# Moving the layer-norm gradient behind the state sums in a fused S4 and feed-forward gradient kernel

## The chip, the cores and the metric

One Trainium2 chip, and one of its cores. The metric is the device time of one execution of the kernel in microseconds. In what follows PE is the matrix engine, DVE the vector engine, ACT the scalar engine, POOL the GpSimd engine and SP the sync engine, which here issues most of the DMAs. Each engine runs its instructions in the order of its own queue.

## The reference

The kernel computes a block and all its gradients: a layer norm, whose result goes through a long convolution with an S4 state-space kernel and, beside it, through a feed-forward layer that gates it. The input has 2048 rows of 512, the feed-forward layer has 1792 units, and the state has 128 entries per channel.

```python
xn = _layernorm(x)                     # x = A_u, 2048 x 512
K  = einsum("dn,dnl,dn->dl", Cc, exp(logdA[:, :, None] * l), dB).real
s  = causal convolution of xn with K, by FFT  + xn * Dskip
g  = silu(silu(xn @ w1) @ w2)          # 512 -> 1792 -> 512
out = x + s * g
# returned: out, and the gradients of A_u, A_re, A_im, B_re, B_im, C_re, C_im, log_dt, Dskip, w1, w2
```

The change touches three parts of the gradient. The *state sums* turn the gradient of `K` into those of A, B, C and `log_dt`. The *weight gradients* are those of `w2` and `w1`, two products over all 2048 rows. The *norm gradient* adds up the two gradients that reach `xn` (from the convolution and from the feed-forward layer), takes them through the layer norm, and adds the gradient that came in: with y the summed gradient of a row, its result is `rstd * (y - mean(y) - xn * mean(y * xn)) + grad_out`.

## The kernel before, in words

The kernel is written as Python generators. Each `yield` ends a *step*, and helpers mix the steps of several generators: `interleave` gives each generator a number of steps per round, `paced(gen, other, rate)` runs `rate` steps of `other` for each step of `gen`, and `chained` runs generators one after another. What comes out is an order of priority. The framework that builds the program then puts the instructions of each engine in order by this priority and by when it reckons that each is ready, so that the queues keep the order of the steps only roughly. It also adds the waits on semaphores. Tiles with a tag rotate through `bufs` buffers, and a new use of a buffer waits for the last reader of the old one. A pool that is opened in memory of a closed pool waits in the same manner, tile by tile.

The forward part, the gradient of the convolution and the gradient through the feed-forward layer (`gen_ffn_da`) come first and are not changed. The state sums start beside `gen_ffn_da`. In the profiled execution the last call of the kernel function, line 1147, takes over at about 545 us. It mixes three things:

- `gen_ssm_bwd` (L825), the state sums, 16 groups in all, of which about ten are still to come. For each group, `ssm_turned` (L722) loads `YT` with two DMA transposes on SP; `ssm_v` (L729) makes 16 matmuls, which ACT evicts to `Vb` in four pieces; `ssm_products` (L742) forms `Tp` by four multiplications on DVE; and `ssm_sums` (L752) adds up `Tp` by 43 matmuls with an identity, evicted by ACT to `Sa`. A group's matmuls are placed one step, its products one group, and its sums two groups after it has begun. For every second group `ssm_half` (L711) makes `Gb` on DVE and loads `Eb`; for every fourth, `ssm_fold` (L682) loads `GE` and makes `Gf`. After every fourth group `gen_ssm_grads` (L766) turns `Sa` into the gradients of A, B, C and `log_dt`: some 45 small DVE instructions, six PE transposes (`pt_g`, L813), a matmul for `log_dt` (`pd`, L818), one more DVE instruction (`ddt`, L820), and stores on POOL.
- `gen_dw2` (L911) and then `gen_dw1` (L943), the weight gradients. Each of 14 steps of `gen_dw2` loads an `h_in` (512 KB, SP), transposes one in 16 PE instructions (`pt_t`, L118), applies SiLU on ACT to make `a_tok` (two instructions), multiplies in 16 matmuls of 512 columns (L936), evicts on ACT to `o11`, and stores on POOL. `gen_dw1` loads, for each of 7 blocks, a `dh_tok` by two DMA transposes on SP (L949; two buffers), and makes four steps of 16 matmuls of 256 columns each (L954), evicts each on ACT, and stores the block on POOL. All these evictions are line 44 in the profile, and these products share three PSUM buffers. The profile calls both output tiles `o`, as it does the `o1` below.
- `gen_ln_bwd` (L961), the norm gradient, in 8 chunks of 256 rows. `load` fetches `du` (gradient from the convolution), `pd_l` (from the feed-forward layer) and `Gt` (the incoming gradient), 256 KB each, on SP. `sums` forms the sum and the two means on DVE (L983, L984, each twice, and a short L985) and scales the sum on ACT (L988, twice). `rows` puts the result together on DVE (L994 twice, L995) and stores it on POOL (L996). `rows` of a chunk follows `sums` of the next.

```python
    interleave([ssm, chained([gen_dw2(k, fw), gen_dw1(k, fw)]), after(8, gen_ln_bwd(k, fw))], [2, 1, 2])
```

The round is two steps of the state sums, one of the weight gradients and two of the norm gradient, which is held back for eight steps. The norm gradient therefore runs out after 13 rounds, in the middle of the state sums; the state sums end while `gen_dw1` is at its first block; and the other 27 steps of `gen_dw1`'s 28 run with nothing beside them. All tiles of the norm gradient lie in the pool `fw`, beside those of the weight gradients. The tiles of the state sums lie in `sb`, on the other side of the memory, which stays open until the kernel ends.

Of the kernel before, what the change touches and what calls it, by code (L numbers as in the profile page):

```python
# [13 lines left out]
BF16 = mybir.dt.bfloat16  # L14
# [3 lines left out]
P = 128  # L18
# [29 lines left out]
def interleave(gens, weights=None):  # L48
    gens = list(gens)
    weights = list(weights or [1] * len(gens))  # L50
    alive = [True] * len(gens)
    while any(alive):
        for i, g in enumerate(gens):
            if not alive[i]:
                continue
            for _ in range(weights[i]):
                try:
                    next(g)
                except StopIteration:
                    alive[i] = False  # L60
                    break
# [16 lines left out]
def chained(gens):  # L78
    for g in gens:
        yield from g  # L80


def after(n, g):
    for _ in range(n):
        yield
    yield from g
# [9 lines left out]
def paced(gen, other, rate):  # L96

    n = 0.0
    for _ in gen:
        n += rate  # L100
        while n >= 1:
            next(other, None)
            n -= 1
# [9 lines left out]
def turned(k, src, n, out, ev):  # L113

    for i in range(0, n, 8):
        pt = k.pf.tile([P, 8, P], BF16, name="pt_t", tag="pf")
        for j in range(8):
            k.nc.tensor.transpose(out=pt[:, j], in_=src(i + j), identity=k.ident[:])  # L118
        ev(out[:, i:i + 8], pt[:])
# [705 lines left out]
def gen_ssm_bwd(k, sb):  # L825


    par = load_params(k, sb, 0, k.D)
    par["dt"] = k.dt[:]
    groups = [(b, h, q0) for b in range(4) for h in range(2) for q0 in (0, 8)]  # L830
    gf, half, yt, vb, tp, S, tail = {}, {}, {}, {}, {}, {}, []
    gf[0] = ssm_fold(k, 0, sb)
    yt[0] = ssm_turned(k, *groups[0], sb)
    yield
    n = len(groups)
    for i in range(n + 2):
        if i < n:
            b, h, q0 = groups[i]
            if q0 == 0:
                half[i // 2] = ssm_half(k, b, h, gf[b], sb)  # L840
            if i + 1 < n:
                yt[i + 1] = ssm_turned(k, *groups[i + 1], sb)
            vb[i] = ssm_v(k, q0, half[i // 2][0], yt.pop(i), sb)
            if (i % 4) == 2 and b < 3:
                gf[b + 1] = ssm_fold(k, b + 1, sb)
            yield
        if i >= 2:
            j = i - 2
            b, h, q0 = groups[j]
            if (j % 4) == 0:  # L850
                S[b] = sb.tile([P, 3, 32, 2, 4], F32, name="Sa", tag="Sa", bufs=2)
            ssm_sums(k, tp.pop(j), S[b][:, :, 16 * h + q0:16 * h + q0 + 8])
            yield
            if (j % 4) == 3:
                tail.append(gen_ssm_grads(k, b, S.pop(b), par, sb))
        if 1 <= i <= n:
            tp[i - 1] = ssm_products(k, groups[i - 1][2], vb.pop(i - 1), half[(i - 1) // 2][1], sb)
            yield
        if tail:
            if next(tail[0], "end") == "end":  # L860
                tail.pop(0)
    for t in tail:
        yield from t
# [47 lines left out]
def gen_dw2(k, fw):  # L911
    nc = k.nc

    def load(ft):
        h = fw.tile([P, k.T, P], BF16, name="h_in", tag="h_in", bufs=2)
        nc.sync.dma_start(h[:].rearrange("p t n -> p (t n)"), k.Hd[ft])
        return h

    def turn(h):
        a = fw.tile([P, k.T, P], BF16, name="a_tok", tag="a_tok", bufs=2)  # L920
        turned(k, lambda t: h[:, t], k.T, a, lambda out, in_: nc.scalar.activation(out=out, in_=in_, func=ACT.Silu))
        return a
    h = load(0)
    yield
    a = turn(h)
    h = load(1)
    yield
    for ft in range(k.FT):
        at = a
        if ft + 1 < k.FT:  # L930
            a = turn(h)
            if ft + 2 < k.FT:
                h = load(ft + 2)
        ps = k.pf.tile([P, k.D], F32, name="ps_w2", tag="pf")
        for t in range(k.T):
            nc.tensor.matmul(out=ps[:], lhsT=at[:, t, :], rhs=k.do[:, t, :], start=(t == 0), stop=(t == k.T - 1))  # L936
        ob = fw.tile([P, k.D], BF16, name="o11", tag="o11", bufs=2)
        k.evb(ob[:], ps[:])
        k.st(k.outs[11][ft * P:ft * P + P, :], ob[:])  # L939
        yield  # L940


def gen_dw1(k, fw):  # L943
    nc = k.nc
    o10 = k.outs[10].rearrange("(k p) f -> p k f", p=P)
    for f in range(k.FT // 2):
        dh = fw.tile([P, k.T, 2, P], BF16, name="dh_tok", tag="dh_tok", bufs=2)
        for j in range(2):
            nc.sync.dma_start_transpose(dh[:, :, j, :], k.DHd[2 * f + j])  # L949
        ob = fw.tile([P, k.DK, 256], BF16, name="o10", tag="o10", bufs=2)  # L950
        for dk in range(k.DK):
            ps = k.pf.tile([P, 256], F32, name="ps_w1", tag="pf")
            for t in range(k.T):
                nc.tensor.matmul(out=ps[:], lhsT=k.xn[:, t, dk * P:dk * P + P], rhs=dh[:, t].rearrange("p j n -> p (j n)"),  # L954
                                 start=(t == 0), stop=(t == k.T - 1))
            k.evb(ob[:, dk], ps[:])
            yield
        k.st(o10[:, :, 256 * f:256 * f + 256], ob[:])  # L958


def gen_ln_bwd(k, lw):  # L961
    nc = k.nc
    TT, STT = nc.vector.tensor_tensor, nc.vector.scalar_tensor_tensor
    D = k.D
    n = k.T // 2
    cols = lambda ap: ap.rearrange("p (b d) -> p b d", b=4)

    def load(c):
        du = lw.tile([P, 4, 2, P], BF16, name="du", tag="du", bufs=3)
        nc.sync.dma_start(du[:].rearrange("p b t d -> p b (t d)"), k.dUd[:, :, 256 * c:256 * c + 256].rearrange("b p n -> p b n"))  # L970
        pd = lw.tile([P, 2, D], BF16, name="pd_l", tag="pd_l", bufs=3)
        nc.sync.dma_start(pd[:], k.Pd[:, 2 * c:2 * c + 2, :])
        Gt = lw.tile([P, 2, D], BF16, name="Gt", tag="Gt", bufs=2)
        nc.sync.dma_start(Gt[:], k.g_v[:, 2 * c:2 * c + 2, :])
        return du, pd, Gt

    def sums(c, du, pd, Gt):

        m = lw.tile([P, 2, 4], F32, name="m", tag="m", bufs=2)
        for i in range(2):  # L980
            t = 2 * c + i
            jk = lw.tile([P, D], BF16, name="jk", tag="jk", bufs=1)
            STT(out=cols(pd[:, i]), in0=cols(pd[:, i]), scalar=1.0, in1=du[:, :, i, :], op0=ALU.mult, op1=ALU.add, accum_out=m[:, i, 0:1])  # L983
            STT(out=jk[:], in0=pd[:, i], scalar=1.0, in1=k.xn[:, t, :], op0=ALU.mult, op1=ALU.mult, accum_out=m[:, i, 1:2])  # L984
        STT(out=m[:, :, 2:4], in0=m[:, :, 0:2], scalar=-1.0 / D,  # L985
            in1=k.rstd[:, 2 * c:2 * c + 2].unsqueeze(2).to_broadcast([P, 2, 2]), op0=ALU.mult, op1=ALU.mult)
        for i in range(2):
            nc.scalar.activation(out=pd[:, i], in_=pd[:, i], func=ACT.Identity, scale=k.rstd[:, 2 * c + i:2 * c + i + 1], bias=m[:, i, 2:3])  # L988
        return pd, Gt, m

    def rows(c, pd, Gt, m):
        o1 = lw.tile([P, 2, D], BF16, name="o1", tag="o1", bufs=2)
        for i in range(2):
            STT(out=o1[:, i], in0=k.xn[:, 2 * c + i, :], scalar=m[:, i, 3:4], in1=Gt[:, i], op0=ALU.mult, op1=ALU.add)  # L994
        TT(out=o1[:], in0=o1[:], in1=pd[:], op=ALU.add)  # L995
        k.st(k.o1_v[:, 2 * c:2 * c + 2, :], o1[:])  # L996
    q, pend = [load(0)], None
    for c in range(n + 1):
        if c + 1 < n:
            q.append(load(c + 1))  # L1000
        yield
        cur = sums(c, *q.pop(0)) if c < n else None
        yield
        if pend:
            rows(c - 1, *pend)
        pend = cur


@with_exitstack
def kernel(ctx, tc, A_u, A_A_re, A_A_im, A_B_re, A_B_im, A_C_re, A_C_im, A_log_dt, A_Dskip, B_x, B_w1, B_w2, grad_out,  # L1010
           out_0, out_1, out_2, out_3, out_4, out_5, out_6, out_7, out_8, out_9, out_10, out_11):
    nc = tc.nc
    k = KCtx()
    k.nc, k.tc = nc, tc
    k.outs = [out_0, out_1, out_2, out_3, out_4, out_5, out_6, out_7, out_8, out_9, out_10, out_11]
    L, D, F = A_u.shape[1], A_u.shape[2], B_w1.shape[1]
# [7 lines left out]
    def pool(name, side=None, es=ctx, **kw):  # L1024
        kw.setdefault("bufs", 1)
        return es.enter_context(tc.tile_pool(name=name, side=side, reuse_waits="tile", **kw))
# [111 lines left out]
    ffb = gen_ffn_da(k, da)  # L1138
    paced(bwd, woven([ffb, out], [2, 1]), BR)
    es_x.close()  # L1140
    sb = pool("sb", side="right")
    ssm = gen_ssm_bwd(k, sb)
    paced(ffb, ssm, SR)
    run(out)
    es_d.close()
    fw = pool("fw")
    interleave([ssm, chained([gen_dw2(k, fw), gen_dw1(k, fw)]), after(8, gen_ln_bwd(k, fw))], [2, 1, 2])
# [1 line left out]
_INS = ['A_u', 'A_A_re', 'A_A_im', 'A_B_re', 'A_B_im', 'A_C_re', 'A_C_im', 'A_log_dt', 'A_Dskip', 'B_x', 'B_w1', 'B_w2', 'grad_out']  # L1149
_OUTS = [((1, 2048, 512), 'bfloat16'), ((1, 2048, 512), 'bfloat16'), ((512, 128), 'bfloat16'), ((512, 128), 'bfloat16'), ((512, 128), 'bfloat16'), ((512, 128), 'bfloat16'), ((512, 128), 'bfloat16'), ((512, 128), 'bfloat16'), ((512,), 'bfloat16'), ((512,), 'bfloat16'), ((512, 1792), 'bfloat16'), ((1792, 512), 'bfloat16')]  # L1150
# [25 lines left out]
```

## Time and profile before

| what | value |
|---|---|
| median of 6 runs | 732.91 us (730.46 to 741.04) |
| profiled execution | 734.1 us, of which the profile's span is 732.4 |
| PE busy | 601.7 us (82% of the span), 5500 matmuls |
| DVE busy | 553.3 us (76%) |
| ACT busy | 496.8 us (68%) |
| POOL busy | 100.3 us (14%) |
| mean granted TensorE clock | 0.936 |
| DMA | 159.26 MB, mean 217 GB/s |
| last matmul of `gen_dw1` begins its group of 128 | 710.14 us, for 14.13 us |

All times in the profile count from the start of the span. Matmuls are pipelined: a busy PE need not be at its peak, and a matmul's own duration is longer than the distance from one to the next. For the rate, the length of a whole group is used. Where a line shows an idle time in square brackets, it is the time that the engine stood still ahead of the instruction, with the instruction or DMA that ended it. Such a wait costs the kernel time only if the engine decides when the kernel ends, or if one that does is waiting for it.

### The profile page before, as it was taken

The page shows a single profiled execution, that of the slowest core. Times are in us where ns is not written, and L with a number is a line of the kernel's source. Part 1 is how long each engine was busy: PE and PEld are TensorE (multiplying, and loading weights), DVE is VectorE, ACT ScalarE, POOL GpSimd, SP SyncE. Part 2 cuts the span into 40 slices and gives each one's busy share as a digit, 9 for nine tenths or more (in the row PEclk, how much of TensorE's full clock was granted, in tenths as well). Part 3 has the DMA queues.
Part 4 walks back from the last instruction along what each step waited for, and adds up shares of the span by engine and source line. Part 5 has one row for each costly group of instructions (what it writes and reads, how often), then busy time and mean ns, then how long its engine had stood idle before and what let it go on. Part 6 is the DMA issues. An engine that isn't in the chain of part 4 may idle for free.

```text
span 732.4 us, 13942 instructions
## 1 busy us (share of the span) xinstructions
PE 601.7 (82%) x5500; PEld 433.5 (59%) x5500; DVE 553.3 (76%) x1070; ACT 496.8 (68%) x671; POOL 100.3 (14%) x180
## 2 busy tenths in 40 slices
PE   0667968969999875669798999989897978999895
PEld 0435646555665653445575676758676656666784
DVE  6969996869988749976896999746897897794100
ACT  7768759679889866858788787636746866661211
POOL 2172100000010026200000000000002103102300
PEclk9978989999999995879999999999999989999998
DMA  9877847769679976569988865599979999930872
GB/s 286 316 168 193 271 170 206 271 179 299 251 194 254 351 256 165 193 149 256 322 217 262 239 208 197 151 219 219 213 159 281 258 281 274 228 117 28 160 183 57
DMA packets 207042, 159.26 MB, mean 217 GB/s; under 512 B 129024, under 2 KB 185344, under 8 KB 203392
## 3 DMA queue, kind: packets, MB, share of 16 engines
q1 hardware_dynamic: 193856, 135.29, 70.1%
q0 software_dynamic: 6224, 18.10, 6.9%
q10 hardware_dynamic: 6896, 4.98, 2.2%
q8 instruction: 43, 0.70, 0.4%
q14 instruction: 23, 0.19, 0.1%
HBM read 65.14 MB, written 62.26 MB: 174 GB/s over the span
## 4 chain that ended last, share of the span: by engine, by line
issue 52%; DVE 5%; POOL 4%; DMA 3%; PE 0%; ACT 0%; POOLq 0%; ACTq 0%; SPq 0%; DVEq 0%
DMA out_dram<-o 2%; POOL out_dram L939 1%; DMA Kd<-KE 1%; DVE YD L599 1%; POOL out_dram L816 1%; DMA Gr<-in_grad_out_dram 1%; DVE sp_in L332 1%; DVE ds L595 1%; POOL out_dram L631 1%; POOL out_dram L958 1%; POOL out_dram L996 1%; DVE sp_in L337 0%; POOL g L598 0%; DVE YD L603 0%; DVE YD L601 0%
## 5 line engine op out<-in xcount | busy, mean ns | idle before, releaser
L44 ACT CAST dA<-ps_s 128x1024 bf16<-128x1024 f32 x96 | 94.6, 1040 | 16.3 <-PE ps_s L298 8.7
L310 PE MATMUL ps_i<-I,sp_in 128*128 128x256 bf16 x384 | 55.2, 291 | 17.5 <-ACT dK L44 7.7
L893 PE MATMUL ps_da<-doT,W 128*128 128x256 bf16 x448 | 60.7, 280 | 4.8 <-ACT doT L44 2.9
L541 PE MATMUL ps_h<-XT,W 128*128 128x256 bf16 x448 | 62.4, 290 | 1.5 <-ACT hT L44 0.9
L558 PE MATMUL ps_o<-W,aT 128*128 128x512 bf16 x224 | 57.9, 398 | 3.1 <-ACT aT L549 2.9
L310 PEld LDWEIGHTS <-sp_in 128*128 128x128 bf16 x384 | 38.0, 103 | 33.5 <-DVE sp_in L333 16.7
L44 ACT CAST o<-ps_w 128x256 bf16<-128x256 f32 (+1 forms) x42 | 18.6, 443 | 57.8 <-PE ps_w L954 42.4
L44 ACT CAST dB<-ps_i 128x1024 bf16<-128x1024 f32 x48 | 47.2, 1025 | 15.7 <-PE ps_i L310 13.3
L746 DVE TENSOR_TENSOR Tp<-Vb,Eb 128x1344 bf16<-128x1344 bf16 x64 | 52.4, 852 | 3.9 <-PE psS L762 3.4
L904 PE MATMUL ps_dx<-W,dhT 128*128 128x512 bf16 x224 | 53.8, 379 | 0.0
L893 PEld LDWEIGHTS <-W 128*128 128x128 bf16 x448 | 44.5, 101 | 14.5 <-issue 5.8
L541 PEld LDWEIGHTS <-W 128*128 128x128 bf16 x448 | 45.7, 104 | 12.4 <-issue 2.3
L936 PE MATMUL ps_w<-YD,a_tok 128*128 128x512 bf16 x224 | 52.3, 386 | 0.7 <-ACT o L44 0.7
L954 PE MATMUL ps_w<-dh_tok,xn 128*128 128x256 bf16 x448 | 50.4, 273 | 2.6 <-DMA dh_tok<-DHd 2.2
L895 DVE SCALAR_TENSOR_TENSOR dhT<-dhT,ps_da 128x512 bf16<-128x512 bf16 x56 | 37.6, 682 | 16.3 <-PE ps_da L893 16.0
L44 ACT CAST Vb<-ps_v 128x672 bf16<-128x672 f32 x64 | 42.8, 724 | 9.4 <-PE ps_v L736 9.3
L954 PEld LDWEIGHTS <-xn 128*128 128x128 bf16 x448 | 43.3, 98 | 8.4 <-issue 3.6
L297 PE MATMUL ps_s<-dB,F 128*128 128x512 bf16 x96 | 37.6, 398 | 7.0 <-DMA dB<-dA 4.3
L286 PEld LDWEIGHTS <-TF 128*128 128x128 bf16 x384 | 27.2, 105 | 26.2 <-issue 14.6
L419 ACT ACTIVATE sn<-V 128x1024 bf16<-128x1024 int32 (+3 forms) x40 | 35.1, 898 | 7.1 <-DVE V L417 6.9
L298 PE MATMUL ps_s<-dB,F 128*128 128x512 bf16 x96 | 36.8, 389 | 1.7 <-DMA dB<-dA 1.7
L447 PEld LDWEIGHTS <-YD 128*128 128x128 bf16 x512 | 24.5, 102 | 22.8 <-DVE YD L434 11.8
(220 smaller groups left out, 1371.4 us busy)
## 6 DMA issues: line engine op xcount, KB each, us to landing
Yd<-YD SPq DMA_DIRECT2D x8, 1024.0 KB, 5.8
sp_in<-Ud SPq DMA_DIRECT2D x8, 1024.0 KB, 7.1
h_in<-Hd SPq DMA_DIRECT2D x14, 512.0 KB, 5.0
Ed<-E SPq DMA_DIRECT2D x8, 672.0 KB, 5.1
Eb<-Ed SPq DMA_DIRECT2D x8, 672.0 KB, 5.8
Hd<-hT POOLq DMA_DIRECT2D x8, 512.0 KB, 7.1
Ud<-dA SPq DMA_DIRECT2D x4, 1024.0 KB, 9.4
KXd<-dA SPq DMA_DIRECT2D x4, 1024.0 KB, 6.1
```

The lines of the kernel that those rows point to most:

```text
L44: return self.nc.scalar.copy(out=out, in_=in_)
L297: nc.tensor.matmul(out=ps[:, 4 * u:4 * u + 4], lhsT=F2[:, m0], rhs=B[:, 0, g0:g0 + 4, :], start=True, stop=False)
L298: nc.tensor.matmul(out=ps[:, 4 * u:4 * u + 4], lhsT=F2[:, m1], rhs=B[:, 1, g0:g0 + 4, :], start=False, stop=True)
L310: nc.tensor.matmul(out=ps[:, g], lhsT=Y[:, c, g0 + g, :], rhs=k.I2[:, c].rearrange("p c m -> p (c m)"), start=(c == 0), stop=(c == 1))
L541: nc.tensor.matmul(out=ps[:, j], lhsT=k.W1[:, dk, ft * P:ft * P + P], rhs=XTv[:, :, dk, :], start=(dk == 0), stop=(dk == DK - 1))
L558: nc.tensor.matmul(out=ps[:], lhsT=aT[:, ft, t * P:t * P + P], rhs=k.W2[:, ft, :], start=(ft == 0), stop=(ft == FT - 1))
L746: k.nc.vector.tensor_tensor(out=Tp[:, c, :, r ^ c].rearrange("p e (q w) a -> p q w e a", w=2), in0=Vb[:, :, c].rearrange("p q w (e a) -> p ...
L893: nc.tensor.matmul(out=ps[:, j], lhsT=k.W2[:, ft, dk * P:dk * P + P], rhs=dTv[:, :, dk, :], start=(dk == 0), stop=(dk == DK - 1))
L895: nc.vector.scalar_tensor_tensor(out=dh[:, i0:i0 + 2, :], in0=dh[:, i0:i0 + 2, :], scalar=1.0, in1=ps[:], op0=ALU.add, op1=ALU.mult)
L904: nc.tensor.matmul(out=ps[:], lhsT=dhs[ft // 8][:, ft % 8, t * P:t * P + P], rhs=k.W1[:, :, ft * P:ft * P + P], start=(ft == 0), stop=(ft ...
L936: nc.tensor.matmul(out=ps[:], lhsT=at[:, t, :], rhs=k.do[:, t, :], start=(t == 0), stop=(t == k.T - 1))
L954: nc.tensor.matmul(out=ps[:], lhsT=k.xn[:, t, dk * P:dk * P + P], rhs=dh[:, t].rearrange("p j n -> p (j n)"), start=(t == 0), stop=(t == k ...
```

## The change

The weight gradients are no longer mixed with the other two in one `interleave`. They are paced beside the state sums at 0.35 steps per step. With the steps as they are, 11 of the 14 steps of `gen_dw2` that transpose are placed before the end of the state sums, and the last of these comes after the last parameter gradient. Then the pool `sb` is closed, and a pool `lw` is opened in its memory for the norm gradient. The norm gradient is mixed, one step for one, with the rest of the weight gradients: the last part of `gen_dw2` and all 28 steps of `gen_dw1`. It has more buffers (`du` and `pd_l` four instead of three, `Gt` four instead of two), it starts with the loads of two chunks, and the load of chunk `c + 2` is placed after `rows(c - 1)`, where the load of chunk `c + 1` was placed ahead of the step before.

```diff
     def load(c):
-        du = lw.tile([P, 4, 2, P], BF16, name="du", tag="du", bufs=3)
+        du = lw.tile([P, 4, 2, P], BF16, name="du", tag="du", bufs=4)
         nc.sync.dma_start(du[:].rearrange("p b t d -> p b (t d)"), k.dUd[:, :, 256 * c:256 * c + 256].rearrange("b p n -> p b n"))
-        pd = lw.tile([P, 2, D], BF16, name="pd_l", tag="pd_l", bufs=3)
+        pd = lw.tile([P, 2, D], BF16, name="pd_l", tag="pd_l", bufs=4)
         nc.sync.dma_start(pd[:], k.Pd[:, 2 * c:2 * c + 2, :])
-        Gt = lw.tile([P, 2, D], BF16, name="Gt", tag="Gt", bufs=2)
+        Gt = lw.tile([P, 2, D], BF16, name="Gt", tag="Gt", bufs=4)
         nc.sync.dma_start(Gt[:], k.g_v[:, 2 * c:2 * c + 2, :])
         return du, pd, Gt
...
-    q, pend = [load(0)], None
+    q, pend = [load(0), load(1)], None
     for c in range(n + 1):
-        if c + 1 < n:
-            q.append(load(c + 1))
         yield
         cur = sums(c, *q.pop(0)) if c < n else None
         yield
         if pend:
             rows(c - 1, *pend)
         pend = cur
+        if c + 2 < n:
+            q.append(load(c + 2))
...
     es_x.close()
-    sb = pool("sb", side="right")
+    es_b = ctx.enter_context(ExitStack())
+    sb = pool("sb", side="right", es=es_b)
     ssm = gen_ssm_bwd(k, sb)
     paced(ffb, ssm, SR)
     run(out)
     es_d.close()
     fw = pool("fw")
-    interleave([ssm, chained([gen_dw2(k, fw), gen_dw1(k, fw)]), after(8, gen_ln_bwd(k, fw))], [2, 1, 2])
+    dw = chained([gen_dw2(k, fw), gen_dw1(k, fw)])
+    paced(ssm, dw, 0.35)
+    es_b.close()
+    interleave([gen_ln_bwd(k, pool("lw", side="right")), dw], [1, 1])
```

## The prediction

> **What bounds the kernel now.** I first read the rows of the 40 slices on the page: the change touches only the last quarter, slices 30 to 39, where PE is at 8 or 9 tenths throughout while DVE runs full and then falls to nothing.
>
> ```profile
> PE   0667968969999875669798999989897978999895
> DVE  6969996869988749976896999746897897794100
> PEclk9978989999999995879999999999999989999998
> DMA  9877847769679976569988865599979999930872
> ```
>
> Then the busy time by stretches. The columns are the stretch, its length, busy us of PE, PE weight load, DVE, ACT and POOL (with instructions), the granted TensorE clock, the DMA share and GB/s. 545 is where the last `interleave` (L1147) begins to run, 562:640 holds the norm gradient, 680:724 is `gen_dw1` alone.
>
> ```profile
> 545.00:562.00 17.00, 13.65 (x163) 11.25 (x161) 12.66 (x25) 10.21 (x14) 0.00 (x0) 0.90 1.00 256
> 562.00:640.00 78.00, 68.87 (x686) 48.71 (x684) 65.33 (x163) 54.67 (x78) 16.61 (x31) 0.93 1.11 267
> 640.00:668.00 28.00, 27.59 (x297) 19.29 (x295) 17.96 (x52) 14.49 (x22) 6.26 (x12) 1.00 0.28 91
> 668.00:680.00 12.00, 9.94 (x99) 7.88 (x97) 9.84 (x38) 2.51 (x6) 0.87 (x3) 1.00 0.04 14
> 680.00:724.00 44.00, 41.40 (x376) 36.49 (x376) 0.28 (x1) 8.57 (x23) 7.49 (x12) 1.00 0.74 160
> ```
>
> PE decides the end: it runs to 724.3, and only an eviction and the store (8 us) follow. The sum of its work can't change, so the change is worth what PE gaps it closes, less those it opens. Between 640 and 668, with the state sums and the weight gradient but no norm gradient, PE is busy 27.6 of 28 us; between 562 and 640, with the norm gradient, it loses 9.1 us and some clock. The timeline says why. First PE, then ACT, then DVE, each row with start, length, and in brackets the idle time ahead of it and what ended it:
>
> ```profile
> 594.03 0.72 PE L118 MATMUL pt_t<-ident,h_in 128*128 128x128 bf16 x10
> 599.42 0.72 PE L736 MATMUL ps_v<-Gb,YT 128*128 128x168 bf16 x4 [4.67 <-ACT Vb L44]
> 601.13 4.93 PE L936 MATMUL ps_w<-YD,a_tok 128*128 128x512 bf16 x16
> 609.14 3.62 PE L936 MATMUL ps_w<-YD,a_tok 128*128 128x512 bf16 x16
> 617.31 0.28 PE L758 MATMUL psS<-Tp,ident 128*128 128x128 bf16 x2 [1.85 <-DVE ddt L820]
> 635.49 3.61 PE L936 MATMUL ps_w<-YD,a_tok 128*128 128x512 bf16 x16 [0.71 <-ACT o L44]
> ...
> 596.76 1.52 ACT L988 ACTIVATE pd_l<-pd_l,m,rstd 128x512 bf16<-128x512 bf16 x2 [4.53 <-DVE m L985]
> 598.66 1.33 ACT L44 CAST Vb<-ps_v 128x672 bf16<-128x672 f32 x2
> ...
> 616.36 0.69 DVE L983 SCALAR_TENSOR_TENSOR pd_l<-pd_l,du 128x512 bf16<-128x512 bf16 x1 [1.85 <-DMA pd_l<-Pd]
> 616.98 0.27 DVE L820 TENSOR_TENSOR ddt<-pd,dt 1x128 bf16<-1x128 f32 x1
> ```
>
> The longest PE gap is the norm gradient's: its L988 stood on ACT waiting 4.53 us for its sums on a crowded DVE, with the evictions of `ps_v` behind it. The 1.85 us gap too: its L983 waited for `pd_l`, and `ddt`, which PE waited for, stood behind it on DVE.
>
> **The change, part by part.** The norm gradient costs DVE 16 x (0.69 + 0.08) for L983, as much for L984, 16 x 0.745 for L994, 8 x 0.68 for L995 and 8 x 0.16 for L985: 43.2 us; ACT 16 x 0.81 = 13 us; DMA 8 x (3 x 256 KB in, 256 KB out) = 8.4 MB, some 31 us of all engines at the 267 GB/s of the 562:640 row. All of it moves from the stretch that starts at 545 to the one beside the last weight gradients.
>
> *Taken away (a).* PE gaps that the norm gradient caused: 4.67, 1.85, a 0.51 at 564.2 of the kind of the 1.85, and 0.71 at 635.5, where ACT stood in L988 just before: 7.7 us. I let all go, since 640:668 shows the regime that is left: one weight-gradient step per group of state sums, DVE full, PE gaps of 0.2 us. What is late next is the ready time of `Vb` and `Tp`, with per group (4 products of 0.85, half a `Gb` of 1.55, a quarter of the 9.8 us parameter gradient) 6.6 us of DVE against 8.3 us of PE (16 + 43 small matmuls and a step of L936).
>
> *Taken away (b), the clock after those gaps.* The L936 group at 601.13 takes 4.93 for 3.62 us, and the small ones beside it 0.9 more; after the 1.85 us gap, groups of 2.23 and 1.63 us stand where 1.2 and 1.28 are usual, and 0.4 more: 2.2 + 1.8 = 4.0 us. The Trainium skill ("TensorE: Matmul & The Clock Gate", Part 1) says that PE falls to half clock after an idle window of about 3.4 us and needs 3.4 us of work to come back. By that rule the short gap costs no clock and the long one 1.7 us. The trace has a clock loss after both, so I take 4.0; by the rule the whole sum would be 2.3 us worse. The same row warns that a new gap of 2 us may cost twice its length; the 1.58 us gap at 695 (clock 1.00) says it need not.
>
> *Fewer filler steps, `paced(ssm, dw, 0.35)`.* One step per 2.9 steps of the state sums instead of one per 2. Between zero (8.3 us PE against 6.6 DVE and about 6.7 ACT leave room) and 5 us (a parameter gradient that holds a product back in each of three groups). I take +1. At the start (the 2.97 us wait for `h_in` at 552.9, behind 3.8 us of `YT` transposes on SP) `ssm_sums` of group 5 now comes ahead of the first transposes and can fill some: -1, bounds -2 to +2.
>
> *The end of the state sums.* After the last sums PE needs the last parameter gradient: DVE 669.35 to 679.5, 10.2 us. Today `gen_dw1` fills it but for 2.1 us. Then it is five L936 steps (4.4 us each with their transposes) that must be pulled ahead, and the third needs an `h_in` whose SP issue stands next to the norm gradient's first loads; these wait for memory that the parameters hold until that gradient is over. `dh_tok` was issued at 596 today, far ahead of its place in the code, so the order on a queue is by readiness, and I take +1; bounds 0 and +9 (SP stands until the gradient is over, and PE with it).
>
> *Beside the last weight gradients.* PE is left with about 22 us of L936 and 49.4 us of L954 after the state sums; the norm gradient is 8 us of loads and 43 of DVE, so it ends some 12 us or more before PE. DVE's 43 us are hidden there, PE needs nothing of it. But three things can reach PE:
> - ACT in order: an L988 that waits holds the evictions of `ps_w`, one per 1.75 us. Three PSUM buffers give 3.5 us; the longest such wait now is 4.53. +1, bounds 0 and 8 (all 10.0 us of L988's waits, less a little).
> - POOL in order: the `o1` stores wait for L995 (17.4 us in all, longest 11.0) with `o11`/`o10` stores behind; those have two buffers, 8 us of PE. 0, or +3.
> - DMA. The 680:724 stretch is the row to look at: with nothing beside the transposes the DMA share is already 0.74, and PE waits 0.43 + 1.58 + 0.59 us:
>
> ```profile
> 686.69 7.15 PE L954 MATMUL ps_w<-dh_tok,xn 128*128 128x256 bf16 x64 [0.43 <-ACT o L44]
> 695.42 14.13 PE L954 MATMUL ps_w<-dh_tok,xn 128*128 128x256 bf16 x128 [1.58 <-DMA dh_tok<-DHd]
> 710.14 14.13 PE L954 MATMUL ps_w<-dh_tok,xn 128*128 128x256 bf16 x128 [0.59 <-DMA dh_tok<-DHd]
> ```
>
> A pair of transposes may start when its buffer is free and has one step of 64 matmuls, 7.06 us. 0.74 x 44 = 32.6 us of DMA for ten, less some 5 stores of 0.9, is 2.8 us each, 5.6 a pair. The loads of chunks 0 to 3 come before the first such pair, those of chunks 4 to 7 (one per 5.4 us of DVE) fall on it and the two after, each with a store: 1.05 MB at 267 GB/s, 3.9 us. 9.5 - 7.06 is 2.4 late, three times: +7. Here a rule of the Trainium skill speaks against the change too: DMAs of different engines run on the same 16 DMA engines and interleave ("DMA: Bandwidth & Descriptors", Issuing engines are not separate DMA queues), so the stores on POOL do not pass by. The page's 261 GB/s for a transpose (Latency and other measured facts) would make a pair 4.0 us and the lateness 0.9, three times: +3, an estimate. The upper bound is the four transposes issued at 596 to 632 beside these very loads: 4.7 us median on SP against 2.6 alone, 4.2 more a pair, three times: +13. Between 3 and 13 I take +6, near the solo row, since PE's own delay lets the loads get ahead.
>
> Sum: -7.7 - 4.0 + 1 - 1 + 1 + 1 + 6 = -3.7 us. The profiled execution took 734.1 (span 732.4), 1.2 above the median of 732.9: 730.4 in its own time, 729.2 by the median. I say 729.
>
> **The rivals.** A difference under 1% (7.3 us) can't be told from none here.
> - *The transfers fit (faster).* The transposes cost 2, the fillers and the end 1 in all: -11.7 - 1 + 3 = -10, 723. For it: DMA idles at 0.28 and 0.04 from 640 to 680 today, and two pairs of `dh_tok` are loaded far ahead. Against: 0.74 with PE waiting, in just the place where 31 us are added. 0.35.
> - *About half is given back*, as in the sum: 729, own range 726 to 738. 0.37.
> - *Transposes behind the norm gradient's traffic (slower).* Place: `dh_tok` of the third to fifth pair; price 13 us and clock after each gap of 2 us or more, three times 1.7: 18, with the other terms +3 and -12.7 taken off: +8, 741. It decides once a pair needs over 11 us, that is once transposes go at the 4.7 us of 596:632. For it: that row. Against: `YT` transposes shared the queue there, and are gone by then. 0.28.
> - That the norm gradient isn't hidden at all but sets the end would need it to run 12 us or more late; it is inside the last.
>
> **How the numbers follow.** Likeliest 729. The faster case reaches down to 717 (all gaps of 545 to 680 gone), the slower to 750; leaving out a tenth on each side gives 718 to 744. Faster by over 1% (below 725.6) 0.35; within 1% 0.37; slower (above 740.2) 0.28.
>
> **What will show it.** (a, b) right: no L988 between the `Vb` evictions, no PE gap over 1 us and a clock of 1.00 from 562 until the state sums end, which come some 25 us earlier; wrong: gaps before `ps_v` or `psS` by `Vb` or `Tp`. End of the sums: gap of PE before `pt_g`, or before `pt_t` by `h_in`. DMA: PE's total wait for `dh_tok` (2.2 us today) at 5 to 9, and a DMA share near 1 beside the last weight gradients. The prediction fails if that wait stays at 3, or passes 12, or if PE waits for `ps_w` evictions behind L988 for more than 3 us.

## The result, and the profile after

The changed kernel took 732.08 us (median of 35 runs, 722.68 to 737.84) against 733.86 for the kernel before (72 runs beside them, 726.01 to 741.04). The ratio is 0.9968, 95% interval 0.995 to 0.9985: 0.3% or 2.3 us faster, clear of zero, and far inside the 1% that a few runs can tell. The medians are of all runs; the ratio leaves out, on both sides, the runs that took over 1.5% more than the fastest of their kernel. Ratios are used below, because the kernel before moved between 732.7 and 735.5 from one group of runs to the next; "us by the ratio" is a ratio times 733.

The profiled execution took 730.06 us (span 728.3). Again the busy time by stretches: stretch, length, busy us of PE, PE weight load, DVE, ACT and POOL with instructions, granted clock, DMA share, GB/s. The norm gradient now runs from 649 to 697.

```profile
562.00:640.00 78.00, 74.08 (x836) 54.61 (x834) 50.24 (x132) 47.27 (x69) 12.31 (x23) 1.00 0.79 175
640.00:659.00 19.00, 17.43 (x114) 8.81 (x115) 12.27 (x42) 9.75 (x13) 5.85 (x11) 1.00 0.75 247
659.00:673.00 14.00, 14.00 (x129) 12.40 (x127) 13.87 (x39) 7.32 (x15) 2.92 (x5) 1.00 0.90 231
673.00:681.00 8.00, 0.74 (x6) 0.46 (x5) 7.97 (x21) 1.66 (x3) 1.84 (x3) 0.76 1.14 319
681.00:698.00 17.00, 15.42 (x128) 13.01 (x127) 8.18 (x20) 7.12 (x14) 3.14 (x5) 0.91 0.89 197
698.00:720.00 22.00, 20.84 (x192) 18.41 (x190) 0.00 (x0) 4.10 (x11) 1.51 (x2) 1.00 0.67 131
```

Against the rows of before: from 562 to 640 PE does 74.1 us of work instead of 68.9 and holds its full clock, and the DMA share falls from 1.11 to 0.79. From 673 to 681 PE does nothing, while the DMAs are at 1.14, and the clock falls. The timeline of PE names both places:

```profile
589.47 0.74 PE L736 MATMUL ps_v<-Gb,YT 128*128 128x168 bf16 x8
592.42 0.45 PE L118 MATMUL pt_t<-ident,h_in 128*128 128x128 bf16 x5 [2.21 <-DMA h_in<-Hd]
...
641.37 0.23 PE L813 MATMUL pt_g<-ident,gout 128*128 128x128 bf16 x1 [1.49 <-DVE gout L790]
...
658.97 14.14 PE L954 MATMUL ps_w<-dh_tok,xn 128*128 128x256 bf16 x128
680.37 15.86 PE L954 MATMUL ps_w<-dh_tok,xn 128*128 128x256 bf16 x128 [7.26 <-DMA dh_tok<-DHd]
697.80 7.15 PE L954 MATMUL ps_w<-dh_tok,xn 128*128 128x256 bf16 x64 [1.58 <-DMA dh_tok<-DHd]
706.11 14.13 PE L954 MATMUL ps_w<-dh_tok,xn 128*128 128x256 bf16 x128 [1.16 <-DMA dh_tok<-DHd]
```

The gaps of 4.67 and 1.85 us between the state sums are gone. A gap of 7.26 us stands where the third pair of `dh_tok` is needed, and the group after it takes 15.86 us instead of 14.13: the granted clock fell to 0.50 at about 677, in the gap, and comes back to 1.00 at about 684. SP's queue tells why the pair was late:

```profile
665.62 0.37 SPq L970 DMA_DIRECT2D du<-dUd  x1
666.15 4.33 SPq L949 DMA_TRANSPOSE dh_tok<-DHd  x1
670.58 0.53 SPq L974 DMA_DIRECT2D Gt<-in_grad_out_dram  x1
671.20 0.41 SPq L972 DMA_DIRECT2D pd_l<-Pd  x1
671.66 4.31 SPq L949 DMA_TRANSPOSE dh_tok<-DHd  x1
```

The first transpose is issued at 666.15, when PE has done half of the group of 128 and so left the first buffer. PE needs the pair at 673.1. Each transpose holds SP for 4.3 us, two loads of the norm gradient stand between them, and the second lands at about 680.

### The profile page after: what moved, and what is told of

It reads as the page before. It is cut to its first block, busy times and chain, and to the rows that moved or that the text cites. A ratio compares the mean times of both kernels' runs of the same rounds, so it can differ in the third digit from the quotient of the medians.

```text
span 728.3 us, 13974 instructions
## 1 busy us (share of the span) xinstructions
PE 595.3 (82%) x5500; PEld 428.4 (59%) x5500; DVE 555.0 (76%) x1070; ACT 496.2 (68%) x671; POOL 99.9 (14%) x180
## 4 chain that ended last, share of the span: by engine, by line
issue 52%; POOL 5%; DVE 5%; DMA 2%; PE 0%; ACT 0%; POOLq 0%; ACTq 0%; SPq 0%; DVEq 0%
POOL out_dram L816 1%; POOL out_dram L939 1%; DVE YD L599 1%; DMA Gr<-in_grad_out_dram 1%; DMA out_dram<-gout 1%; DVE sp_in L332 1%; POOL out_dram L958 1%; DMA Kd<-KE 1%; POOL out_dram L631 1%; DVE ds L595 1%; POOL out_dram L996 1%; DVE sp_in L333 0%; POOL g L598 0%; DVE YD L603 0%; DVE YD L601 0%
## 5 line engine op out<-in xcount | busy, mean ns | idle before, releaser
L895 DVE SCALAR_TENSOR_TENSOR dhT<-dhT,ps_da 128x512 bf16<-128x512 bf16 x56 | 37.4, 682 | 15.4 <-PE ps_da L893 15.2
```

What stands on the lines that cost most here:

```text
L895: nc.vector.scalar_tensor_tensor(out=dh[:, i0:i0 + 2, :], in0=dh[:, i0:i0 + 2, :], scalar=1.0, in1=ps[:], op0=ALU.add, op1=ALU.mult)
```

## The experiments

### What the norm gradient costs in each place

The norm gradient was left out of both kernels.

```diff
 # b_noln, from the kernel before
-    interleave([ssm, chained([gen_dw2(k, fw), gen_dw1(k, fw)]), after(8, gen_ln_bwd(k, fw))], [2, 1, 2])
+    interleave([ssm, chained([gen_dw2(k, fw), gen_dw1(k, fw)])], [2, 1])
 # a_noln, from the changed kernel
-    interleave([gen_ln_bwd(k, pool("lw", side="right")), dw], [1, 1])
+    run(dw)
```

> The kernel before with the norm gradient left out altogether (the gradient of A_u is not computed); nothing else differs. Theory (the norm gradient cost PE gaps and clock only, 7.7 + 4.0 us): 11.7 us less than before, about 722, with no PE gap over 1 us and no half clock between 562 and the end of the state sums. Rival (the gaps belong to the state sums themselves and another wait takes their place): less than 5 us saved. The third reading, that the norm gradient also slowed the transfers, shows as more than 14 us saved.

> The changed kernel with the norm gradient left out (the gradient of A_u is not computed). Theory (in its new place the norm gradient costs 7.26 + 1.58 + 1.16 us of PE waits for dh_tok, less some 2.6 that were there before, and 1.7 us of half clock, about 9 us): the kernel falls by 9 us, to about 722 to 723, the same as the kernel before without it. Rival (the wait for dh_tok is that of two buffers and comes whatever runs beside it): it falls by less than 3 us.

Measured: b_noln 721.47 us, ratio to before 0.9851 (0.9814 to 0.9889); a_noln 719.32 us, 0.9841 (0.9799 to 0.9884). Both theories held. In PE's timeline of b_noln, no gap over 0.5 us is left between the wait for the first `h_in` and the end of the sums, and the clock is 1.00 (last row, by stretches); the gaps at both ends are what the kernel before had too:

```profile
554.51 1.89 PE L118 MATMUL pt_t<-ident,h_in 128*128 128x128 bf16 x16 [3.22 <-DMA h_in<-Hd]
664.95 0.23 PE L813 MATMUL pt_g<-ident,gout 128*128 128x128 bf16 x1 [1.54 <-DVE gout L790]
...
562.00:657.00 95.00, 92.47 (x969) 65.70 (x980) 47.99 (x117) 58.42 (x84) 18.23 (x34) 1.00 0.71 166
```

This divides the result into two parts. In its old place the norm gradient cost 0.0149, 10.9 us by the ratio (8.1 to 13.6). In its new place it costs 0.9968 - 0.9841 = 0.0127, 9.3 us, by the two intervals some 6 to 13. The rest of the change, pace and order without a norm gradient, is 0.9841 against 0.9851, nothing that these runs can tell. -10.9 + 9.3 - 0.7 are the -2.3 us.

### What makes the third pair of transposes late

First, the three loads of the norm gradient were issued by POOL, so that SP has nothing between the transposes.

```diff
 # a_pool: in load() of gen_ln_bwd, for du, pd_l and Gt
-        nc.sync.dma_start(
+        nc.gpsimd.dma_start(
```

> The changed kernel with the three loads of the norm gradient issued by POOL instead of SP. Theory (the transposes are slow because all queues share the DMA engines): the wait of PE for dh_tok stays within 3 us of 7.3, and the time within 3 us of the changed kernel. Rival (the transposes are slow because loads stand between them on SP and use up its issue time): the pair is issued in two transposes of 2.6 us without loads between, the wait falls below 3 us and the time by 5 us or more.

Neither held: 742.39 us, ratio 1.0139 (1.0104 to 1.0174), and the wait grew.

```profile
696.22 16.16 PE L954 MATMUL ps_w<-dh_tok,xn 128*128 128x256 bf16 x128 [18.58 <-DMA dh_tok<-DHd]
```

The rival had the mechanism wrong: from 668.6 to 698.7 SP issued nothing but transposes, four of them, and the pair still took until 696. My theory, that the engines are shared, was on the right side, but it took the queue to make no difference. Time from issue to landing (median us, last column, in the stretch in which the third pair was moved) was, with the loads on SP as in the changed kernel, with the loads on POOL, and without a norm gradient:

```profile
pd_l<-Pd SPq DMA_DIRECT2D x2, 256.0 KB, 4.9
dh_tok<-DHd SPq DMA_TRANSPOSE x3, 8.6
```

```profile
pd_l<-Pd POOLq DMA_DIRECT2D x3, 256.0 KB, 16.2
dh_tok<-DHd SPq DMA_TRANSPOSE x4, 15.4
```

```profile
dh_tok<-DHd SPq DMA_TRANSPOSE x3, 5.6
```

On SP's queue a load takes its turn between transposes; from a second queue the loads run at the same time as they do, and both sides become slow. More loads then fall on the pair as well: POOL issued eight in the 12 us after the pair's first issue, SP four in 14 us. The profile also lists POOL's queue as another kind (software, where SP's is hardware). How much is due to the number of loads, to the second queue as such and to its kind, this run doesn't tell. Next, the traffic itself was taken away: the loads of chunks 4 to 7, then also the stores.

```diff
 # a_half; kept lists the tiles of chunks 0 to 3
+        if c >= 4:
+            return kept[c - 4]
...
+        kept.append((du, pd, Gt))
 # a_half_nost, besides
-        k.st(k.o1_v[:, 2 * c:2 * c + 2, :], o1[:])
+        if c == 7:
+            k.st(k.o1_v[:, 2 * c:2 * c + 2, :], o1[:])
```

> The changed kernel without the loads of chunks 4 to 7 of the norm gradient; these chunks are computed on the tiles of chunks 0 to 3, so that half of the gradient of A_u is other numbers. All arithmetic and all stores stay. Theory (it is the traffic of these loads, 3 MB, that makes the third pair of transposes late): the pair is issued at about the same time as in the changed kernel, lands in about 8 us instead of 14, the wait of 7.3 us falls below 2 and the time by 6 to 9 us. Rival (the lateness comes from the start of the issue, when a buffer comes free, and not from traffic): the wait stays above 5 us. If the stores and the DVE's work were the cause, it also stays above 5.

> As a_half (no loads for chunks 4 to 7), and of the norm gradient's stores only the last is left, so that seven eighths of the gradient of A_u are not written. The DVE and ACT work stays. Theory (what was left of the wait, 3.7 and 3.9 us in a_half, comes from the stores on POOL, which share the DMA engines with the transposes): both waits fall to about 1 us as without the norm gradient, and the time by 4 to 7 us against a_half. Rival (the remaining waits come from the late issue or from DVE's reads): the waits stay at 3 us or more.

Without these loads: 728.22 us, ratio 0.9889 (0.984 to 0.9938), 5.8 us by the ratio below the changed kernel. Without the stores too: 722.77 us, 0.9861 (0.9824 to 0.9899). PE's waits for `dh_tok` in the two, first a_half, then a_half_nost:

```profile
678.71 15.79 PE L954 MATMUL ps_w<-dh_tok,xn 128*128 128x256 bf16 x128 [3.72 <-DMA dh_tok<-DHd]
698.42 15.80 PE L954 MATMUL ps_w<-dh_tok,xn 128*128 128x256 bf16 x128 [3.92 <-DMA dh_tok<-DHd]
```

```profile
675.38 7.15 PE L954 MATMUL ps_w<-dh_tok,xn 128*128 128x256 bf16 x64 [0.75 <-DMA dh_tok<-DHd]
684.66 15.75 PE L954 MATMUL ps_w<-dh_tok,xn 128*128 128x256 bf16 x128 [2.13 <-DMA dh_tok<-DHd]
```

The first wait goes from 7.26 to 3.72 to 0.75 us: about half of it belongs to the loads of the later chunks, and half to the `o1` stores on POOL, which my expectation of a_half (below 2) had left out. The loads' part is clear in the time as well; that of the stores (0.3%) is seen only in the waits of one trace each, since the two intervals overlap. The first issue is equally late in all three (666.2, 668.0, 667.7 us, 7 us ahead of PE's need), so it is the traffic that makes the difference between them. Part of the wait moved to a later pair: all waits for `dh_tok` sum to 10.0, 8.3 and 4.0 us. a_half's trace is of its slowest run (731.83 us) and has half clock after two gaps, so it does not show where the 5.8 us of its median come from.

### The other parts of the change

The first of these changes is shortened to what differs.

```diff
 # a_bufs: the buffers of before (a_fw builds on it)
-du bufs=4, pd_l bufs=4, Gt bufs=4
+du bufs=3, pd_l bufs=3, Gt bufs=2
 # a_fw, besides
-    interleave([gen_ln_bwd(k, pool("lw", side="right")), dw], [1, 1])
+    interleave([gen_ln_bwd(k, fw), dw], [1, 1])
 # a_r50, from the changed kernel
-    paced(ssm, dw, 0.35)
+    paced(ssm, dw, 0.5)
```

> The changed kernel with the buffer counts of the norm gradient as before (du and pd_l three, Gt two). Theory (only the place of the traffic matters): the loads come a little later, fewer of them before the third pair of transposes and more beside it and the fourth, the waits for dh_tok sum to 10 to 14 us against 10.0, time 0 to 4 us above the changed kernel. Rival (more buffers only let more loads in ahead of the transposes): the first wait falls below 5 us and the time by 2 us or more.

> As the one before (three, three and two buffers), but with the norm gradient's tiles in the pool of the weight gradients instead of the memory that the state sums free. Theory (the memory of the state sums keeps the loads back until the last parameter gradient has ended, at 643 us): the loads of the first chunks are issued earlier, in the stretch of the state sums where the DMAs have room, and the norm gradient ends earlier; fewer loads then meet the transposes, the wait for dh_tok falls to 3 to 6 us and the time is 2 to 6 us below that kernel. Rival (the norm gradient then comes back between the state sums and their gaps come back): PE gaps by L988 before Vb, and no gain.

> The changed kernel with the weight gradients paced at 0.5 instead of 0.35 beside the state sums. Theory (the pace matters little while PE is full; it only shifts steps of the weight gradient from behind the state sums to between them): PE gaps between 562 and the end of the state sums stay below 0.5 us each, but behind the state sums PE has some 6 steps of L936 less (about 20 us), so the third pair of transposes meets the first loads instead of the fifth and later: waits for dh_tok of 10 to 18 us, time 0 to 6 us above the changed kernel. Rival (0.35 leaves PE short of work between the sums): the time falls by 2 us or more.

*a_bufs*: 734.89 us, 1.0012 (0.998 to 1.0043). Its waits for `dh_tok` sum to 9.6 us, against 10.0, so the expected shift of the traffic didn't show there; it has a longer wait for `h_in` (3.01 us at 595.6). The extra buffers may be worth some 0.4%, 3 us, but the two intervals just overlap.

*a_fw*: 744.04 us, 1.0109 (1.0061 to 1.0157). The rival. PE's waits for `dh_tok` are down to 2.0 us in all, but the norm gradient, no longer kept back by memory, has come forward between the state sums. ACT and PE there:

```profile
618.34 0.81 ACT L988 ACTIVATE pd_l<-pd_l,m,rstd 128x512 bf16<-128x512 bf16 x1 [11.09 <-DVE m L985]
```

```profile
619.41 1.22 PE L758 MATMUL psS<-Tp,ident 128*128 128x128 bf16 x10 [6.48 <-ACT Sa L763]
```

It is the gap of the kernel before, larger: L988 waits 11.09 us for its sums, and the eviction `Sa` behind it keeps PE. With the same buffers in the memory of the state sums (a_bufs) this doesn't happen. So the place in the code doesn't put the norm gradient behind the state sums; the memory does, by the wait on the tiles of the state sums.

*a_r50*: 748.02 us, 1.0178 (1.0133 to 1.0222), beyond what theory or rival gave: the waits for `dh_tok` sum to 25.0 us. Without a norm gradient the pace made no difference that can be told; with it, it moves the transposes in SP's queue. The third pair got through, and then SP stood in the loads: the last three of those ahead of the fourth pair, and PE's wait for it:

```profile
686.15 0.32 SPq L972 DMA_DIRECT2D pd_l<-Pd  x1
686.51 1.23 SPq L970 DMA_DIRECT2D du<-dUd  x2
687.84 5.39 SPq L949 DMA_TRANSPOSE dh_tok<-DHd  x1
```

```profile
703.00 15.79 PE L954 MATMUL ps_w<-dh_tok,xn 128*128 128x256 bf16 x128 [19.61 <-DMA dh_tok<-DHd]
```

From 671.66 to 687.74 SP issued loads alone, 17 of them, the later ones with idle time ahead as buffers came free one by one, and the transposes stood behind. That the place on SP, and not the traffic, makes most of these 19.6 us is read from the queue; it wasn't tried by itself.

### A version that is faster than both

A third buffer lets the third pair be loaded beside the state sums. The move took the norm gradient's 21 KB per partition out of `fw`; a third buffer takes 8. No run has a third buffer in the kernel before, where it would bring `fw` to 67.1 KB; the waits for `dh_tok` that it could take away there are 2.2 us.

```diff
-        dh = fw.tile([P, k.T, 2, P], BF16, name="dh_tok", tag="dh_tok", bufs=2)
+        dh = fw.tile([P, k.T, 2, P], BF16, name="dh_tok", tag="dh_tok", bufs=3)   # a_dh3; a_dh4 has 4
 # a_dh3_h3 and a_dh4_h3, besides
-        h = fw.tile([P, k.T, P], BF16, name="h_in", tag="h_in", bufs=2)
+        h = fw.tile([P, k.T, P], BF16, name="h_in", tag="h_in", bufs=3)
```

> The changed kernel with three buffers for dh_tok instead of two. Theory (the third pair of transposes is late because it can't be issued until 666 us and then meets the loads of the norm gradient): it is issued in the stretch of the state sums, where the DMAs have room (share 0.79), the wait of 7.26 us and its clock loss go: 7 to 9 us less than the changed kernel, about 723. Rival (the DMAs are full from there to the end, so that the wait moves to the next pairs): waits for dh_tok still sum to 7 us or more, and the time falls by less than 3 us.

> The changed kernel with four buffers for dh_tok. Theory (each pair that is loaded before the state sums end is one that doesn't meet the norm gradient's traffic): the wait of 3.9 us that three buffers leave (684 us) goes, 3 to 5 us less than with three, about 0.979 of before. Rival (the transposes that are put ahead in the stretch of the state sums stand before h_in and YT on SP and open gaps there, as the 1.8 and 1.7 us at 590 to 600 with three buffers): the same time as with three, within 2 us.

> Three buffers for dh_tok and three for h_in. Theory (h_in is late at 590 us because its issue waits for a buffer and then stands behind transposes on SP): the gap before the transposes of h_in goes, 1 to 3 us less than with two buffers for h_in. Rival (SP is in order, and an earlier h_in only pushes YT back): no difference within 2 us.

> Four buffers for dh_tok and three for h_in. If both theories hold: 0.975 to 0.98 of before, about 716 us; if both rivals hold: as with three and two, 0.984.

| kernel | `dh_tok`, `h_in` buffers | median us | ratio to before | PE waits for `dh_tok`, us | for `YT`, us |
|---|---|---|---|---|---|
| changed kernel | 2, 2 | 732.08 | 0.9968 (0.995 to 0.9985) | 10.0 | 0 |
| a_dh3 | 3, 2 | 723.10 | 0.9844 (0.9793 to 0.9896) | 3.9 | 2.3 |
| a_dh3_h3 | 3, 3 | 723.40 | 0.9868 (0.983 to 0.9906) | 1.8 | 2.2 |
| a_dh4 | 4, 2 | 727.62 | 0.9927 (0.9899 to 0.9955) | 0 | 4.0 |
| a_dh4_h3 | 4, 3 | 724.03 | 0.9893 (0.9856 to 0.993) | 0 | 4.5 |

Three buffers do what was expected in the time: 1.24%, 9 us by the ratio, off the changed kernel, with 3.9 us of the waits still left. A fourth takes these away too, and yet the time is 0.8% above that with three, worse than even the rival had it; the intervals lie just apart, and overlap with three `h_in`. The transposes that are put ahead stand before `YT` and `h_in` on SP, and PE waits among the state sums: in a_dh4 4.0 us for `YT` and 3.6 for `h_in` (2.3 and 1.3 in a_dh3), with the granted clock at 0.50 after two of these gaps. a_dh4's longest wait for `YT`:

```profile
612.08 0.32 PE L736 MATMUL ps_v<-Gb,YT 128*128 128x168 bf16 x1 [2.44 <-DMA YT<-Yd]
```

A third `h_in` closes its gap at 590, but beside three `dh_tok` makes no difference in time that the intervals show.

## Why the prediction was right or wrong

The forecast was a gain of 3.7 us, 729 us, with "within 1%" the likeliest. That class is right, but the gain is 2.3 us, because one term of the sum, what the transfers cost in the new place, was put at 6 us and measured 9.3 to 9.5. That the total came within 1.4 us is in part luck: the four small terms, put at +2 together, came out at about -0.7 (within some 4 us), which hid much of it. The steps:

- *Gaps taken away and their clock, -7.7 and -4.0:* right. Leaving the norm gradient out of the kernel before gains 10.9 us by the ratio (8.1 to 13.6), and the clock is 1.00 from 562 to 640 there and in the changed kernel. By the idle window of about 3.4 us that the Trainium skill gives ("TensorE: Matmul & The Clock Gate", Part 1) the two would have been 9.4 together, an estimate. The time can't tell 9.4 from 11.7, but the granted clock can: in the kernel before it stands at 0.50 from 617.5 to 620.5, after the gap of 1.85 us. It was right to take the loss from the trace; what goes with it is in the last section.
- *Fewer filler steps +1, the start -1:* together nothing that the two kernels without a norm gradient show. The first wait for `h_in` fell from 2.97 to 1.55 us, and the clock of 0.50 after it, from 553 to 556, is gone. Not foreseen: 2.21 us for `h_in` at 592, behind a `dh_tok` transpose that was put ahead on SP and took 5.83 us.
- *The end of the state sums, +1:* 1.49 us of gap where there was 1.53, plus some tenths on either side. The fillers were pulled ahead as hoped.
- *ACT +1 and POOL 0:* nothing reached PE from either. L988 waited 3.5 us in all instead of 10.0: it waits for DVE, which has nothing else to do there.
- *DMA +6:* the step that failed, in the sentence "Between 3 and 13 I take +6, near the solo row, since PE's own delay lets the loads get ahead". The trace has 10.0 us of waits for `dh_tok` instead of 2.2, and 1.7 of clock that was priced only in the slower rival: 9.5. What was priced as 2.4 us on each of three pairs came as 7.26 on the first, because four loads, of two chunks, and the stores of three met that one pair. The transposes took 4.33 and 4.31 us on SP, so the row to use was the contended one (4.7), which stood in the sum as its upper bound. Counted on three pairs it would have been too much (a sum of +3.3 us before any clock); with the measured 9.5 in place of 6 the sum is -0.2.
- *The rule on shared engines* (the Trainium skill, "DMA: Bandwidth & Descriptors", Issuing engines are not separate DMA queues), weighed against the change, held: the stores on POOL made half of the first wait. The page's 261 GB/s for a transpose (Latency and other measured facts), 2 us for 512 KB, would have put the price at 3, an estimate; the two transposes that counted took 4.3 us each on SP.

Of its own signs, the wait for `dh_tok` at 10.0 us lies above the 5 to 9 that it named, and one gap over 1 us was left among the state sums, the 2.21 for `h_in`. One reading was loose: in the slices 30 to 39 PE stands at 7 to 9 and last at 5, and DVE at 7 to 9 before it falls; no term rests on it.

Of the rivals, "the transfers fit" (723 us) is what the kernel becomes with the third buffer (723.10), not by itself. "Transposes behind the norm gradient's traffic" named the right place and asked for 11 us a pair to decide; the first pair took 14, but only that one.

## What to carry to other kernels

When work is moved out from between engines that it holds up, price its transfers where they land, at the durations that the trace shows under contention and not at those measured alone. A transfer that is needed soon after its buffer comes free is the one that pays; a buffer more, out of memory that the move has freed, can be worth several times the move itself (9 us against 2.3), until the early transfers stand in front of something else. In a program whose queues are ordered by readiness, as here, the place in the code does not fix where work runs; the memory that it had to wait for did.

## What was not expected of the hardware

Loads issued on a second queue, POOL's, beside DMA transposes slowed the transposes more than the loads on the transposes' own queue did: 15.4 us from issue to landing against 8.6, and 5.6 with neither. More of the loads met the transposes that way.

Short gaps of PE can halve its clock, and the price does not follow the length of the gap. Groups of 128 matmuls took 15.75 to 15.86 us, instead of 14.13, after gaps of 2.13, 3.72, 3.92, 7.26 and 19.61 us, and 16.16 after 18.58. Gaps of 1.85 us (the kernel before) and 1.89 (a_noln) were followed by a clock of 0.50, but gaps of 2.21 (the changed kernel, at 592) and 2.37 (a_half, at 594) were not. The records of the granted clock show what goes with it: the clock changes only at steps of 3.41 us, and it follows how much of the step before PE was busy. First two steps of the kernel before, then two of the changed kernel:

```profile
614.02:617.43 3.41, 1.40 (x18) 1.06 (x19) 1.56 (x5) 2.02 (x4) 3.25 (x7) 1.00 0.83 245
617.43:620.85 3.42, 3.42 (x35) 3.42 (x34) 3.00 (x9) 2.03 (x3) 0.74 (x3) 0.50 1.15 230
```

```profile
588.35:591.76 3.41, 1.86 (x19) 1.18 (x17) 0.14 (x1) 2.38 (x4) 1.25 (x3) 1.00 1.05 270
591.76:595.18 3.42, 2.76 (x42) 2.44 (x43) 0.28 (x1) 1.38 (x4) 2.98 (x6) 1.00 1.21 250
```

With PE busy for 1.40 us of a step (41%) the next step had half clock, with 1.86 (54%) it had not. In the 2819 such steps of all 14 traces, a step at full clock in which PE was busy for less than 40% was followed by half clock in all 148 cases, one with 50% or more in none of 2238, and one in between in 45 of 77. Back from half clock, it took more: none of 127 steps under 70% was followed by full clock, and 186 of 190 with 80% or more were. (Ends of matmuls are modelled, so the shares are not exact.) So a gap of about 2 us cost clock where most of it lay in one step, and nothing where it lay across two.
